# Attention and feed-forward block on one core: two tiles of exponentials in one ScalarE instruction where no dense item holds a bank, and a rearranged end

## The chip, the cores and the metric

The kernel runs on one core of one Trainium2 chip. The core has five engines with queues of their own: TensorE (PE, the matrix engine), VectorE (DVE), ScalarE (ACT), GpSimd (POOL) and SyncE (SP, which issues the DMAs). The matrix engine writes into PSUM, which has eight banks of 512 fp32 values on each of 128 partitions. The metric is the device time of one execution in microseconds; three runs of the kernel before gave a median of 1225.08 us (1224.64 to 1225.44).

## The reference

A pre-norm block on 2048 tokens of width 512. Attention has 32 heads of 16 columns; the feed-forward part is 1792 wide. All inputs are bfloat16.

```python
x = A_x                                    # (1, 2048, 512)
# attention on layernorm(x)
scores = einsum("bhqd,bhkd->bhqk", q, k) * 16 ** -0.5
p = softmax(scores);  o = einsum("bhqk,bhkd->bhqd", p, v)
h  = x + o.reshape(B, S, D) @ wo
# feed-forward on layernorm(h)
h2 = h + (gelu(hn @ w_gate) * (hn @ w_up)) @ w_down
```

The scores are 32 x 2048 x 2048 values, 134 million. Each of them is written into PSUM twice: once so that its row's maximum can be taken, and once more, shifted by that maximum, for the exponential.

## The kernel before, in words

**Two passes over the scores.** The work is cut into 64 units of four heads and 256 queries (or eight heads and 128 queries in the last 16 units), and each unit into 16 steps, called ticks. In one tick, pass one has PE write two banks of raw scores (`p1_pair`, L852, two matmuls of 512 columns) and DVE take the row maxima of both banks in one instruction of 1024 columns (`p1_consume`, L867). Pass two is 24 ticks behind, on a unit whose maxima are known. In the same tick PE writes two tiles of shifted scores, one bank each (`p2_tile`, L943, two or four matmuls for a tile), and ACT takes one exponential per tile, 128 x 512 from PSUM to a ring of 34 bf16 tiles in SBUF, called PTM, PTE and PTG (`p2_consume`, L972). Later PE multiplies these tiles with the values (`item_pv`, L989), ACT copies the sums out (OB), and a DMA and GpSimd finish the division.

**Fourteen units take one tick less.** In the units listed in `JOINT`, the maxima of the last two key chunks of one pair are taken together: PE writes a difference of scores into a bank (`item_diff`, L1075 and L1077), ACT takes its relu into SBUF (RB, L1080), and DVE adds it back while it reduces (L864, twice in such a unit). One tick of pass one falls away.

**Dense items run beside it.** Projections, the output projection, the gate, up and down matmuls and the PV sums are generators in a list. The class `Dense` takes one at a time and advances it by a piece or so per tick. An item holds one PSUM bank from its start until its result has been copied out, most often by ACT (`evac_act`, L696). In a tick with no dense work PE gets two filler matmuls instead (`dummy`, L1587).

**Banks.** Pass one uses banks 0 to 3 in two pairs. Pass two and the dense items share banks 4 to 7 through a first-in, first-out list, `banks.free`. A tile takes the bank at the front; when the instruction that reads it is written down, the bank goes to the back of the list. In the program a bank can thus be handed on before its reader has run, and PE waits for that reader by a semaphore.

**Order and waits.** The Python program writes down, tick by tick, one list of instructions for each engine. Each engine executes its list strictly in order. Waits are worked out from what each instruction reads and writes. The two matmuls of pass one and the first tile of pass two are one group (`group_begin`, `group_end`): all their waits are moved ahead of the group's first matmul. In a tick, PE's list is: the group, the second tile, then the dense piece or the fillers. ACT's list is: the exponentials, then the copy of a dense item that has just ended, then whatever was deferred (tanh, squares).

**The planner's costs.** `act_lag` is an account of how far ACT should be behind. Each tick adds 0.478 us per exponential and subtracts 1.135; a copy adds 0.48. Dense items start, and the tanh instructions are placed, only while the account is low enough (`LAG_START`, `LAG_OP`, `LAG_TH`). Nothing of it waits at run time: it sets the order alone.

**The end.** When pass one is over (tick 1024), the last 40 or so tiles of exponentials are done in pairs, 128 x 1024 in one instruction (`p2_pair`, L960). Then `tail_b` finishes the last token tile: the division, output projection, second norm, gate and up with the hardware's gelu, and down.

Of the kernel before, what the change touches and what calls it, by code (L numbers as in the profile page):

```python
# [209 lines left out]
ACT = mybir.ActivationFunctionType  # L210
# [5 lines left out]
NFC = F // 128  # L216
# [5 lines left out]
PV_T = (15, 16, 17, 18)  # L222
PV_TL = (9, 10, 17, 18)
DOWN_AT = 2
A_LATE = True
GH = 6
# [13 lines left out]
J_AT, J_GONE = 10, 14  # L240
LAG_EXTRA = 0.3
POLY = 1.3
TICK = 1.135
# [4 lines left out]
def bass_sequential_preLN__mha_block__geglu_ffn__prompt_kernel(nc, A_x, A_wqkv, A_wo, B_x, B_w_gate, B_w_up, B_w_down, out):  # L248
    dbg = None
    with ExitStack() as es:  # L250
# [288 lines left out]
        class Dense:  # L539
            def __init__(self):  # L540
                self.prio = []
                self.ready = []
                self.extra = []
                self.gen = None
                self.bank = None
                self.banks = [7, 3, 4, 5]
                self.rr = 0
                self.pause = 0
                self.single = False
                self.done = 0  # L550
                self.now = 0
# [15 lines left out]
            def piece(self):  # L567
                if self.single and self.pause > 0:
                    return 0
                while True:  # L570
# [17 lines left out]
                    try:  # L588
                        cost = next(self.gen)
                        if isinstance(cost, tuple):  # L590
                            if self.single:
                                self.pause = cost[1]
                            if ticking[0]:
                                return 0
                            continue
                        return cost
                    except StopIteration as fin:
                        self.gen = None
                        self.done += 1
                        if self.single:  # L600
                            banks.give(self.bank)
                            self.pause = 0 if dve_free[0] else PAUSE
                        return fin.value
            def busy(self):
                return bool(self.gen is not None or self.ready or self.prio)
# [10 lines left out]
        def defer(k, fn):  # L616
            deferred.append((dense.now + k, fn))
# [330 lines left out]
        def p2_pair(ui, tiles):  # L948
# [12 lines left out]
            else:  # L961
                for b, pi in ((b0, q0), (b1, q1)):
                    P.op("act", lambda e, b=b, pi=pi: e.activation(out=PTt(pi), in_=pbank[:, b, :], func=ACT.Exp), reads=[("pb", b)], writes=[("PT", pi)])

        def p2_consume(ui, tiles):
            for (b, m, g) in tiles:
                pi = pt_n[0] % NPT; pt_n[0] += 1
                assert pi not in pt_busy, "PT ring too small"
                pt_busy.add(pi)
                pt_of[(ui, m, g)] = pi  # L970
                dX = rdeps("M", [(n_, i_) for n_ in ("QKE", "QKE2") for i_ in range(5)]) if NPT_M - 10 <= pi < NPT_M else rdeps("E", [("xn", t) for t in range(NT)]) if NPT_M <= pi < NPT_M + NPT_E else (rdeps("G", [("x", cc) for cc in range(NCH)]) if pi >= NPT_M + NPT_E else ())
                P.op("act", lambda e, b=b, pi=pi: e.activation(out=PTt(pi), in_=pbank[:, b, :], func=ACT.Exp), reads=[("pb", b)], writes=[("PT", pi)], extra_deps=dX)  # L972
                banks.give(b)
# [216 lines left out]
        def item_oprojA(b):  # L1190
# [7 lines left out]
            P.op("pe", lambda e: e.matmul(pbank[:, b, :], ident[:], hh, start=False, stop=True), reads=["ident", ("h", GL % 2, 0)], writes=[("pb", b)], sig=True)  # L1198
            P.op("dve", lambda e: e.bn_stats(out=stats2[:, t, :], in_=pbank[:, b, :]), reads=[("pb", b)], writes=[("stats2", t)])
            P.op("dve", lambda e: e.tensor_copy(out=hh, in_=pbank[:, b, :]), reads=[("pb", b)], writes=[("h", GL % 2, 0)])  # L1200
            P.op("dve", lambda e: e.bn_aggr(out=mv2[:, t, :], in_=stats2[:, t, :]), reads=[("stats2", t)], writes=[("mv2", t)])
            P.op("dve", lambda e: e.tensor_scalar(out=rstd2[:, tt], in0=mv2[:, tt, 1], scalar1=EPS, scalar2=None, op0=ALU.add), reads=[("mv2", t)], writes=[("rstd2", t)])
# [7 lines left out]
        def item_hnA(b):  # L1210
            pt = pbank[:, b, :].bitcast(BF16)
            for dc in range(4):
                P.op("pe", lambda e, dc=dc: e.transpose(out=pt[:, 128 * dc:128 * dc + 128], in_=hn_sb[:, 0, 128 * dc:128 * dc + 128], identity=ident[:]),
                     reads=[("OH", 0), "ident"], writes=[("pb", b)], sig=(dc == 3))
            P.op("dve", lambda e: e.tensor_copy(out=hnT_l[GL % 2][:, :, 0:128], in_=pt[:, 0:512].rearrange("p (c s) -> p c s", c=4)), reads=[("pb", b)], writes=[("hnT", GL % 2, 0)])
            add_raw()
            return 1
            yield
# [299 lines left out]
        def tail_b():  # L1518
# [7 lines left out]
            for t in range(NTL):  # L1526
                raw_gelu(t)
            raw_mult(0)
            while not a_done[0]:
                fill(1)  # L1530
# [12 lines left out]
            P.op("pool", lambda e: e.tensor_tensor(out=rstd2[:, tt], in0=rstd2[:, tt], in1=nhalf[:, 0:1], op=ALU.pow), reads=[("rstd2", t1), "nhalf"], writes=[("rstd2", t1)])  # L1543
            raw_mult(1, "dve")
            raw_mult(2)
            raw_mult(3)
            P.op("dve", lambda e: e.tensor_scalar(out=hn_sb[:, 1, :], in0=g_h(GL, 1), scalar1=mv2[:, t1, 0:1], scalar2=rstd2[:, tt], op0=ALU.subtract, op1=ALU.mult),
                 reads=[("h", 1, 1), ("mv2", t1), ("rstd2", t1)], writes=[("OH", 1)])
            down_h(0, GL, 0)
            for fc in chunks(0):  # L1550
                down_mm(0, GL, 0, fc)
            fill(FILL_A)
            tail_hnT(2, (0, 1), "act")
            tail_hnT(3, (2, 3), "dve")
            for fc in chunks(1):
                down_mm(0, GL, 0, fc)
# [6 lines left out]
            for t in range(NTL):  # L1563
                tail_gate(gb[2 * t % 5], t)
                tail_up(gb[(2 * t + 1) % 5], t)
                if t == 0:
                    for fc in range(8, NFC):
                        down_mm(0, GL, 0, fc)
                    P.op("act", lambda e: e.activation(out=out_sb[:, 0, :], in_=pbank[:, 0, :], func=ACT.Copy), reads=[("pb", 0)], writes=[("osb", 0)])
                    P.dma("sp", lambda e: e.dma_start(out=outv[:, 2 * GL, :], in_=out_sb[:, 0, :]), ("out", 0), reads=[("osb", 0)], writes=[("outd", 2 * GL)])  # L1570
# [33 lines left out]
        ticking[0] = True  # L1604
        def next_tile():
            n = 2 * t2 - behind[0]
            st, jj = n // 2, n % 2
            ui_ = st // 16
            t = p2_tile(ui_, st % 16, 1 - (st + P2_START) % 2, jj)
            return ui_, t  # L1610
        while True:
# [37 lines left out]
            else:  # L1649
                t1 = p1_pair(tick // 16, tick % 16, gp1) if p1_ok else []  # L1650
                if doubles[0]:
                    p1_next.append(p1_pair((tick + 1) // 16, (tick + 1) % 16, 1 - gp1))
            t2l = [next_tile()] if p2_ok and p1_ok else []
            P.group_end("pe")
            if p2_ok and p1_ok:
                behind[0] -= 1
                t2l.append(next_tile())
                if more:
# [15 lines left out]
            if t1:  # L1674
# [5 lines left out]
                if tick == 16 * NU - 1:  # L1680
                    unit_end(tick // 16)
            for ui_, t in t2l:
                p2_consume(ui_, [t])
# [34 lines left out]
            tick += 1  # L1718
        run_deferred(tick, flush=True)
        dense.now = tick + 16  # L1720
        while len(pv_done) < NU:
# [36 lines left out]
```

## Time and profile before

| what | value |
|---|---|
| median of three runs | 1225.08 us |
| the profiled execution | 1225.74 us, span 1224.0 us |
| ACT busy | 1190.3 us, 97% of the span |
| DVE busy | 1181.1 us, 96% |
| PE busy | 1130.3 us, 92% (774 of its matmuls are fillers) |
| POOL busy | 841.3 us, 69% |
| DVE row maxima, 128 x 1024 (L867) | 996 |
| ACT exponentials 128 x 512 (L972) | 2000 |
| ACT exponentials 128 x 1024 (L960), all after pass one | 22 |

The page counts an instruction from its start to its end. Where instructions of one engine overlap, the mean of a group is longer than the time from one end to the next, and the engine can follow one on another faster than that mean. The chain of waits shows the latter: it lists the pieces of the chain that ended last, in order of time, and leaves the overlap out. "Idle before" of a group is the time in which the engine stood still ahead of its instructions, with what ended it.

### The profile page before, as it was taken

How to read it: one execution, taken by the hardware profiler on the slowest of the kernel's cores; microseconds unless marked ns; L12 is line 12 of the kernel's file. 1: busy time of each engine (PE TensorE's matmuls, PEld its weight loads, DVE VectorE, ACT ScalarE, POOL GpSimd, SP SyncE). 2: the span in 40 equal slices, each digit the busy share in tenths (PEclk: the TensorE clock that was granted, in tenths of full speed). 3: DMA queues.
4: the chain of work that ended last, by engine and by line, in shares of the span. 5: the costliest groups of instructions: out<-in, count | busy, mean ns of one | idle time of the engine just before them, and what ended most of it. 6: DMA issues, size and time to landing. Idle time of an engine off the chain costs nothing.

```text
span 1224.0 us, 36091 instructions
## 1 busy us (share of the span) xinstructions
PE 1130.3 (92%) x14845; PEld 476.7 (39%) x14845; DVE 1181.1 (96%) x1124; ACT 1190.3 (97%) x2421; POOL 841.3 (69%) x1774
## 2 busy tenths in 40 slices
PE   7999998899999999999999999999999999999998
PEld 3233232233333333333332333333334455554565
DVE  8999999999999999999999999999999999999963
ACT  7899999999999999999999999999999999999995
POOL 8567684766776676756868487675767687756762
PEclk9999999999999999999999999999999999999999
DMA  5111104300010000110011000100001100010000
GB/s 153 28 34 27 29 24 136 91 10 9 8 28 21 12 11 8 27 25 8 11 25 14 21 8 10 25 21 15 8 10 27 26 20 13 10 27 13 18 20 15
DMA packets 69651, 32.02 MB, mean 26 GB/s; under 512 B 54768, under 2 KB 68464, under 8 KB 69488
## 3 DMA queue, kind: packets, MB, share of 16 engines
q1 hardware_dynamic: 69488, 29.71, 10.0%
q8 instruction: 118, 1.93, 0.7%
q14 instruction: 45, 0.37, 0.1%
HBM read 11.80 MB, written 2.10 MB: 11 GB/s over the span
## 4 chain that ended last, share of the span: by engine, by line
ACT 56%; DVE 32%; PE 8%; issue 2%; DMA 1%; POOL 1%; POOLq 0%; DVEq 0%
ACT PTM L972 32%; DVE PM L867 31%; ACT PTG L972 10%; ACT PTE L972 5%; PE pbank L1391 2%; ACT th_sb L1262 2%; ACT g_sb L696 2%; ACT u_sb L696 2%; PE pbank L943 1%; PE pbank L852 1%; ACT PTM L960 1%; ACT OB L696 1%; PE pbank L1292 1%; PE pbank L1587 1%; DVE OA L864 1%
## 5 line engine op out<-in xcount | busy, mean ns | idle before, releaser
L867 DVE TENSOR_REDUCE PM<-pbank 128x2 f32<-128x1024 f32 x996 | 1134.9, 1213 | 9.3 <-PE pbank L943 4.4
L972 ACT ACTIVATE PTM<-pbank 128x512 bf16<-128x512 f32 x1357 | 733.0, 718 | 4.4 <-PE pbank L943 1.0
L943 PE MATMUL pbank<-QT,KT 32*128 32x256 bf16 (+1 forms) x5120 | 506.2, 250 | 14.6 <-ACT PTM L972 8.1
L852 PE MATMUL pbank<-KT,QT 32*128 32x512 bf16 x2020 | 388.2, 384 | 25.4 <-DVE PM L867 10.0
L1587 PE MATMUL pbank<-ones_bf,ident 128*128 128x512 bf16 x774 | 237.0, 384 | 29.2 <-ACT PTM L972 4.7
L852 PEld LDWEIGHTS pbank<-KT,QT 32*128 32x128 bf16 x2020 | 97.2, 91 | 351.1 <-DVE PM L867 130.2
L943 PEld LDWEIGHTS pbank<-QT,KT 32*128 32x128 bf16 x5120 | 205.9, 92 | 69.0 <-ACT PTM L972 40.1
L972 ACT ACTIVATE PTG<-pbank 128x512 bf16<-128x512 f32 x407 | 225.1, 710 | 0.8 <-PE pbank L943 0.4
L972 ACT ACTIVATE PTE<-pbank 128x512 bf16<-128x512 f32 x236 | 140.3, 719 | 1.0 <-PE pbank L943 0.7
L989 PE MATMUL pbank<-PTM,VA 128*17 128x256 bf16 (+1 forms) x3470 | 126.0, 252 | 1.6
L1030 POOL TENSOR_TENSOR LINV<-OBT,negone 128x8 f32<-128x8 bf16 x63 | 105.1, 1668 | 6.2 <-DMA OBT<-OB 5.9
L1587 PEld LDWEIGHTS pbank<-ones_bf,ident 128*128 128x128 bf16 x774 | 45.3, 97 | 132.6 <-ACT PTM L972 83.8
L1272 POOL TENSOR_TENSOR th_sb<-g_sb 128x512 f32<-128x512 f32 (+1 forms) x50 | 51.2, 1024 | 63.6 <-ACT g_sb L696 63.6
L989 PEld LDWEIGHTS pbank<-PTM,VA 128*17 128x17 bf16 x3470 | 67.1, 90 | 39.8 <-issue 22.1
L1271 POOL TENSOR_TENSOR th_sb<-th_sb,g_sb 128x512 f32<-128x512 f32 (+1 forms) x50 | 62.4, 1248 | 4.0
L922 POOL TENSOR_TENSOR QT<-QT,STG 128x256 bf16<-128x256 bf16 x64 | 42.8, 668 | 31.8 <-DMA STG<-ST 31.1
L1274 POOL TENSOR_TENSOR th_sb<-th_sb,g_sb 128x512 f32<-128x512 f32 (+1 forms) x50 | 62.3, 1246 | 1.7
L1270 POOL TENSOR_SCALAR th_sb<-th_sb 128x512 f32<-128x512 f32 (+1 forms) x50 | 30.5, 611 | 40.9 <-ACT th_sb L1262 40.7
L1391 PE MATMUL pbank<-wd_sb,GUT 128*128 128x512 bf16 x210 | 57.4, 382 | 1.0 <-DVE OnT L1422 0.3
L767 POOL TENSOR_SCALAR QT<-QKS,qmask 128x512 bf16<-128x512 bf16 x30 | 46.9, 1568 | 13.3 <-ACT QKS L696 11.9
L1347 PE MATMUL pbank<-hnT_l,wg_sb 128*128 128x256 bf16 x336 | 51.2, 275 | 3.3 <-ACT PTM L972 0.7
L1383 POOL TENSOR_TENSOR GUT<-th_sb,u_sb 128x512 bf16<-128x512 f32 x42 | 53.3, 1268 | 1.3
(198 smaller groups left out, 1210.1 us busy)
## 6 DMA issues: line engine op xcount, KB each, us to landing
QKS<-QKS SPq DMA_DIRECT2D x27, 112.0 KB, 2.1
x_sb<-in_A_x_dram SPq DMA_DIRECT2D x4, 512.0 KB, 5.8
xres<-in_A_x_dram SPq DMA_DIRECT2D x16, 128.0 KB, 2.4
out_dram<-out_sb SPq DMA_DIRECT2D x15, 128.0 KB, 1.7
wg_sb<-in_B_w_gate_dram SPq DMA_DIRECT2D x4, 448.0 KB, 4.2
wu_sb<-in_B_w_up_dram SPq DMA_DIRECT2D x4, 448.0 KB, 3.9
wd_sb<-in_B_w_down_dram SPq DMA_DIRECT2D x3, 512.0 KB, 4.5
STG<-ST SPq DMA_TRANSPOSE x64, 2.3
```

What stands on the lines that cost most here:

```text
L696: P.op("act", lambda e: e.activation(out=o_ap, in_=i_ap, func=ACT.Copy, **kw), reads=reads, writes=writes, extra_deps=extra)
L852: P.op("pe", lambda e, g=g, b=b: e.matmul(pbank[:, b, :], QT[32 * g:32 * g + 32, c, slot, 128 * qt:128 * qt + 128], KT[32 * g:32 * g + 32, ...
L867: P.op("dve", lambda e: e.tensor_reduce(out=PM[:, par, qt, kc, g:g + 2], in_=pbank[:, b:b + 2, :], axis=AX.X, op=ALU.max), reads=[("pb", b ...
L943: P.op("pe", lambda e, kt=kt, i=i: e.matmul(pbank[:, b, qn * i:qn * i + qn], KT[32 * g:32 * g + 32, slot, 128 * kt:128 * kt + 128], QT[32 ...
L972: P.op("act", lambda e, b=b, pi=pi: e.activation(out=PTt(pi), in_=pbank[:, b, :], func=ACT.Exp), reads=[("pb", b)], writes=[("PT", pi)], e ...
L989: P.op("pe", lambda e, g=g, kt=kt, pi=pi, i=i, s_=s_, c0=c0, qn=qn: e.matmul(pbank[32 * g:32 * g + 17, b, c0:c0 + qn], VA[:, kt, 4 * s_ + ...
L1030: P.op("pool", lambda e: e.tensor_tensor(out=li, in0=o4[:, :, :, 16], in1=negone[:, 0:4 * nq].rearrange("p (q h) -> p q h", q=nq), op=ALU. ...
L1271: o(1.27, lambda e: e.tensor_tensor(out=ts_, in0=ts_, in1=gs, op=ALU.mult), [("th", par), ("g", par)])], then=done)
L1274: o(1.27, lambda e: e.tensor_tensor(out=ts_, in0=ts_, in1=gs, op=ALU.mult), [("th", par), ("g", par)])], then=poly_done)
L1383: P.op("pool", lambda e: e.tensor_tensor(out=o_ap, in0=shp(ts_), in1=shp(us), op=ALU.mult), reads=[("th", par), ("u", par)], writes=o_keys ...
L1391: P.op("pe", lambda e: e.matmul(pbank[:, b, :], GUT[:, fc, 128 * k:128 * k + 128], wd_sb[:, fc, :], start=first, stop=last), reads=[("GUT" ...
L1587: P.op("pe", lambda e: e.matmul(pbank[:, b, :], ident[:], ones_bf[:, 0:512], start=True, stop=True), reads=["ident", "ones_bf"], writes=[( ...
```

## The change

Five things change.

1. **Pairs of exponentials during pass one.** If no dense item holds a bank when a tick begins, and two neighbouring banks are both in the free list (`pair_banks`), the two tiles of the tick are put into these two, and one ACT instruction of 128 x 1024 reads both (`p2_both`). Where the two places in the ring of SBUF tiles are not side by side, two single instructions are written as before. `pair_banks` looks for the first bank in the list whose neighbour is anywhere in the list.
2. **The planner's account.** Each pair takes 0.05 us off `act_lag` (`PAIR_GAIN`), so that dense items and tanh instructions may be placed earlier.
3. **A second dense item beside a waiting one.** After pass one, when the running item can't go on, another ready item may run next to it (`beside`).
4. **The last unit's sums and the first of the two last token tiles.** The third and fourth PV part of the last unit may start at ticks 14 and 17 instead of 17 and 18. In `item_oprojA` the copy of h comes before the statistics, which now read the copy in SBUF. The raw gate and up items are added one tick later (`defer(1, add_raw)`).
5. **The order in `tail_b`.** One piece of dense work is placed between the ticks and the end (`TAIL_P`). GpSimd multiplies parts 0 and 1 first; DVE takes part 2, and part 3 after the transposes. The down matmuls of the second last token tile are 8, then 4, then 2, where they were 4, 4 and 6.

```diff
-PV_TL = (9, 10, 17, 18)
+PV_TL = (9, 10, 14, 17)
+TAIL_P = 1
+PAIR_GAIN = 0.05
...
                         if isinstance(cost, tuple):
+                            if dve_free[0]:
+                                other_cost = self.beside()
+                                if other_cost:
+                                    return other_cost
...
+        def pair_banks():
+            for b in banks.free:
+                if b ^ 1 in banks.free:
+                    return b & 6
+            return None
+
+        def p2_both(tl):
+            (ua, (b0, ma, ga)), (ub, (b1, mb, gb)) = tl
+            n = pt_n[0] % NPT
+            if n + 1 < NPT and pt_tiles[n][0] is pt_tiles[n + 1][0] and b1 == b0 + 1:
+                (q0, d0), (q1, d1) = place(ua, ma, ga), place(ub, mb, gb)
+                o_ap = pt_tiles[q0][0][:, pt_tiles[q0][1]:pt_tiles[q0][1] + 2, :]
+                P.op("act", lambda e: e.activation(out=o_ap, in_=pbank[:, b0:b0 + 2, :], func=ACT.Exp), reads=[("pb", b0), ("pb", b1)], writes=[("PT", q0), ("PT", q1)], extra_deps=d0 + d1)
+                banks.give(b0)
+                banks.give(b1)
+                act_lag[0] = max(0.0, act_lag[0] - PAIR_GAIN)
+            else:
+                for u_, t_ in tl:
+                    p2_consume(u_, [t_])
...
-            P.op("dve", lambda e: e.bn_stats(out=stats2[:, t, :], in_=pbank[:, b, :]), reads=[("pb", b)], writes=[("stats2", t)])
             P.op("dve", lambda e: e.tensor_copy(out=hh, in_=pbank[:, b, :]), reads=[("pb", b)], writes=[("h", GL % 2, 0)])
+            P.op("dve", lambda e: e.bn_stats(out=stats2[:, t, :], in_=hh), reads=[("h", GL % 2, 0)], writes=[("stats2", t)])
...
-            add_raw()
+            defer(1, add_raw)
...
             raw_mult(0)
+            raw_mult(1)
...
-            raw_mult(1, "dve")
-            raw_mult(2)
-            raw_mult(3)
+            raw_mult(2, "dve")
...
-            for fc in chunks(0):
+            for fc in range(8):
                 down_mm(0, GL, 0, fc)
             fill(FILL_A)
             tail_hnT(2, (0, 1), "act")
             tail_hnT(3, (2, 3), "dve")
-            for fc in chunks(1):
+            raw_mult(3, "dve")
+            for fc in chunks(2):
                 down_mm(0, GL, 0, fc)
...
-                    for fc in range(8, NFC):
+                    for fc in chunks(3):
                         down_mm(0, GL, 0, fc)
...
-            t2l = [next_tile()] if p2_ok and p1_ok else []
+            pb_ = pair_banks() if p2_ok and p1_ok and dense.gen is None and True else None
+            t2l = [next_tile(pb_)] if p2_ok and p1_ok else []
             P.group_end("pe")
             if p2_ok and p1_ok:
                 behind[0] -= 1
-                t2l.append(next_tile())
+                t2l.append(next_tile(None if pb_ is None else pb_ + 1))
...
+            if pb_ is not None:
+                p2_both(t2l[:2])
+                t2l = t2l[2:]
             for ui_, t in t2l:
                 p2_consume(ui_, [t])
```

## The prediction

> **What bounds the kernel now.** I read the page first, then the groups of pass one's stretch, then the chain of waits in order of time. Durations are in us.
>
> ```profile
> PE 1130.3 (92%) x14845; PEld 476.7 (39%) x14845; DVE 1181.1 (96%) x1124; ACT 1190.3 (97%) x2421; POOL 841.3 (69%) x1774
> PEclk9999999999999999999999999999999999999999
> ACT 56%; DVE 32%; PE 8%; issue 2%; DMA 1%; POOL 1%; POOLq 0%; DVEq 0%
> ```
>
> Two engines are full, and the chain goes to and fro between them. DVE's part, asked for from 33.2 (the first of an unbroken row of maxima) to 1177.8 (the last one's end):
>
> ```profile
> L867 DVE TENSOR_REDUCE PM<-pbank 128x2 f32<-128x1024 f32 x984 | 1120.9, 1213 | 8.4 <-PE pbank L943 4.4 <-PE pbank L852 0.8
> L864 DVE CUSTOM_DVE_ANT_0 OA<-pbank,OA 128x512 f32<-128x512 f32 x28 | 18.1, 682 | 0.1
> ```
>
> The unit prices stand in the chain:
>
> ```profile
> 49.40 1.96 ACT PTM L972 x4
> 571.86 0.28 ACT OB L696
> 645.74 34.01 DVE PM L867 x30
> 1188.81 3.66 ACT PTM L960 x4
> ```
>
> A row maximum takes 34.01/30 = 1.13, a single exponential 0.49, a copy of PV sums (OB) 0.28, an exponential over two banks 3.66/4 = 0.915. Copies of gate, up and the relu RB also cost 0.49, a tanh 0.51. The stretch is 1144.6 long, and DVE's work in it is 984 x 1.131 + 28 x 0.608 = 1130.0. So **ACT and PE together hold DVE up by 14.6, and no relief of ACT can give back more than that.** A full unit is 16 x 1.131 = 18.10 of DVE, a joint unit 17.05.
>
> I summed the same by unit, from the order of instructions and these prices, for units 1 to 63: DVE 1125.4, ACT 1118.0, the larger of the two in each unit 1135.1. The trace has 1140.0, so a unit takes what its fuller engine needs, plus 0.08.
>
> What a wait of PE costs its followers is in two more pieces of the chain:
>
> ```profile
> 644.71 0.05 issue
> 644.75 0.60 PE pbank L1587 x2
> 645.36 0.22 PE pbank L852
> 645.58 0.17 PE pbank L943 x3
> ...
> 683.24 0.05 issue
> 683.29 0.30 PE pbank L852
> 683.59 0.36 PE pbank L943 x5
> 683.95 2.54 ACT PTM L972 x5
> ```
>
> In the second, PE's group is released at 683.24 and ACT begins 0.71 later; its five exponentials take 2.54, not 5 x 0.49 = 2.45, so the first costs 0.09 more when ACT stood idle. In the first piece two fillers stand ahead, and DVE starts 1.03 after the release; without them it is about 0.45 to 0.5.
>
> **The change part by part.** *Pairs.* The order of instructions of the changed kernel has 542 pairs in pass one (1084 of 2000 tiles). Each saves 2 x 0.49 - 0.916 = 0.064, in all 34.4 of ACT; with what moves between the engines at the end, ACT's units sum to 1085.1, not 1118.0. With nothing else changed, the larger sums of the units come to 1131.0: only 4 gained, as DVE needs nearly that anyway, and as the account (`PAIR_GAIN`) fills the freed time of many units with dense work that came later before.
>
> The Trainium skill puts another price on the pair: "ScalarE: Activation LUTs", section "What ACT_TABLE_LOAD costs", gives an ACTIVATE 186 ns plus 0.833 ns an element, with 93 ns of overlap back to back. That is 0.520 and 0.946 (an estimate from that page of the Trainium skill), a saving of 0.093, where the rows show 0.49 and 0.915; by it the forecast below would be some 7 lower. I keep the rows.
>
> *The wait that it adds.* Before, a tile takes the bank at the front of the list, so ACT always has two or three instructions (0.98 or more) left to run between the one that freed the bank and the one that needs it refilled. `pair_banks` takes the first bank whose neighbour is free too, and that neighbour may be the bank handed back last. When a dense item has just ended, it is the bank whose copy ACT has not yet done. The order shows it. Tick 170 of the changed kernel ends with ACT's OB copy of bank 6, and tick 171's group opens with a wait for that copy, because it takes banks 6 and 7; before, bank 6 went to tick 172. Counting all ticks, the instruction that frees the bank stands *directly* ahead of the exponential that needs it 124 times (never before): 62 after an OB copy, 28 after a relu RB, 24 after an exponential, 10 after other copies. Nearly all are waits of the group. Queued behind it on PE are both banks of pass one, both tiles and the dense piece; DVE waits for the first, ACT for the second. POOL's maxima and the DMAs follow DVE's step and have slack (POOL is at 69%).
>
> Cost on ACT, if it is the fuller engine: 0.71 + 0.09 = 0.80 from the row, whose group fed a third tile; for two I take 0.75. Nothing can hide it, because ACT has no other instruction in its list. 124 x 0.75 = 93.
>
> Cost on DVE, if ACT is ahead. The group of a step is released by the reduce two steps back; the reduce between covers 1.13 less the path of 0.5 and a start of 0.1, so a slack of 0.5. Counted from the release of the step before, exponentials begin at 0.71, two singles end at 1.78, OB at 2.06. That is 0.93 after the next reduce's end and overshoots the slack by 0.4. A relu behind a pair ends at 0.71 + 1.01 + 0.49 = 2.21, overshoots by 0.58, and when a second follows two steps later the loop (relu, tiles, pair, the other step's pair, relu) is 0.71 + 1.01 + 0.92 + 0.49 = 3.13 against 2.26, 0.87 lost; mean 0.7. After an exponential: 0.1. Others: 0.5. Sum 62 x 0.4 + 28 x 0.7 + 24 x 0.1 + 10 x 0.5 = 51.
>
> *Smaller waits.* 133 further pairs have only one single (0.49) between, and wait 0.1 to 0.27 if ACT is full; 170 have one pair between, and up to 0.28 where fillers stand in the path. A full ACT pays them, an early one does not: 0 to 27 more.
>
> *Dense items.* Number and kind stay; fillers go from 774 to 775. PE gains and loses nothing.
>
> *The end.* After the transposes of the last tile PE has 9 down matmuls and one residual where it had 4, and later 2 where it had 6: 2 x 0.215 = +0.4 on PE's chain to the end. ACT's two idle gaps at 1182 and 1184 (0.40 and 0.48, waiting for L943 behind raw gate matmuls) can go: up to -0.9. DVE's last product and GpSimd's second lie beside other work (POOL is idle from 1199.9 to 1203.9 and DVE for 2.6 after 1209.9). The statistics take 0.59 from SBUF (L395 at 5.94) and 0.70 from PSUM (L1199 at 1179.44): 0.1 at most. I take 0 in all, with ends -2 and +2, a lost tail gap on each side.
>
> **Sum.** For each unit I take the larger of DVE's work plus its stalls and ACT's work plus 0.75 an event: 1205.7 against 1135.1 before, +70.6. If a unit may hand up to 1.0 of ACT's lateness to the next (the slack above, twice), both fall, to 1193.6 and 1127.8: +65.8. I take the latter, as units heavy and light for ACT alternate. The sum is made against the span of 1224.0 in an execution of 1225.74, 0.66 above the median; on the median it is 1225.1 + 66 = 1291.
>
> **The rivals.**
>
> *DVE's stalls alone (ACT always early).* 1125.4 + 51 = 1176.9, +37 against 1140.0 or +42 by the account: 1262 to 1267. For it: long stretches of the chain are DVE alone (34.01 at 645.74). Against: ACT is at 97%, and half the units have 17.4 or more of its work after the change as well.
>
> *The small waits all count.* The account with 0.2, 0.1 and 0.05 for them gives 1233.0, +98: 1323. For it: ACT at the limit never catches up, as a pair with fillers in its path needs 0.05 + 0.60 + 0.5 + 1.0 per two steps, near DVE's own pace. Against: most fall into units where DVE is slower.
>
> *The other side: pairs win.* If copies end so early that the group never waits for them, the 14.6 of DVE's idle time come back, at best 1210; by the account 4, so 1221. It takes a price under 0.04 an event for the account's 4 (124 x 0.04 = 5), or under 0.12 for the whole 14.6. Speaking for it: the planner places copies where ACT has room. Against: the row of 0.71, which is PE's own path and not a matter of room.
>
> *The matrix clock falls.* PE would stand still for 0.5 or so 124 times. If its clock halved for three steps at each, 0.99 of PE work a step would become 1.98 against 1.13: 124 x 3 x 0.85 = 316, 1541. The row PEclk is 9 in all slices, with PE gaps of 0.4 to 0.7 in them already. The Trainium skill, "TensorE: Matmul & The Clock Gate", section "A second HAM failure mode: psum-queue depth-cycling", tells of short idle times between groups that made the clock swing; by that rule this could come, and no row here shows it.
>
> **How the numbers follow.** About 0.2% (2.5 us) can be told from no change. Forecast (+55 to +80) 0.50; DVE's stalls alone 0.22; all small waits 0.19; pairs win 0.05; no change, gains and waits cancelling, 0.02; the clock 0.02. The range goes from 1250 (two thirds of DVE's stalls) to 1325 (all small waits). Faster 0.05, same 0.02, slower 0.93.
>
> **What would show it.** Right: a group L1010 of 542 at a spacing near 0.92; ACT's busy sum falling by 20 or more though the span grows; DVE's idle time before its maxima (L892) up from 9 to 50 or more, released by PE's L877; waits of PE's L877 on ACT's OB (L721) and RB (L1129) that were not there; in the chain OB, then L877, L968, then DVE or ACT. Wrong: L877 waiting for ACT no longer than now, or a pair's spacing over 0.98, which would put the loss on the instruction itself; or a clock below 9.

## The result and the profile after

The changed kernel takes 1384.8 us (median of 4 runs, 1383.3 to 1385.4). The kernel before took 1225.3 us beside it (1224.6 to 1225.9). The ratio is 1.130, with an interval of 1.128 to 1.131: 160 us slower, where 66 were forecast. The profiled execution is 1384.8 us with a span of 1383.1. The end is not the place of it: from the end of the last row maximum (1338.2) to the end of the span it takes 44.9 us, and it took 46.2 before. The loss lies in pass one. From here on durations are in us.

The steps below are the ticks of the kernel's description. The page of the changed kernel, with the engines, the clock that PE was granted, and the shares of the chain of waits:

```profile
PE 1110.1 (80%) x14700; PEld 458.9 (33%) x14846; DVE 1206.0 (87%) x1122; ACT 1221.3 (88%) x1882; POOL 841.7 (61%) x1773
PEclk9999999999999999999999999999999999999999
ACT 59%; PE 36%; issue 3%; DVE 2%; POOL 0%; POOLq 0%
```

The trace lacks the records of 146 of PE's matmuls (14700 against 14846 weight loads), so PE's 80% is a few points low. No engine is full any more. DVE has nearly left the chain (32% before, 2% now), and PE, the least busy of the three, has 36% of it where it had 8%. That is what a ring of waits looks like: each engine stands still while another one does a short thing for it.

The groups of the changed kernel: instructions, busy time and mean ns, then the idle time just ahead of them and what ended it.

```profile
L892 DVE TENSOR_REDUCE PM<-pbank 128x2 f32<-128x1024 f32 x996 | 1160.0, 1217 | 143.7 <-PE pbank L968 136.8
L877 PE MATMUL pbank<-KT,QT 32*128 32x512 bf16 x2020 | 397.5, 394 | 137.5 <-ACT OB L721 52.0
L1010 ACT ACTIVATE PTM<-pbank 128x1024 bf16<-128x1024 f32 x401 | 398.4, 1023 | 67.6 <-PE pbank L968 61.8
```

DVE stood still for 9 ahead of its row maxima before; now it is 144. The maximum needs the raw scores of L877, which wait for ACT's copies: 137.5 idle ahead of L877, 52.0 of it ended by the OB copy, in the view of waits in 62 places.

```profile
PE pbank L877 <- ACT OB L721: 52.0, 62, 1.3
PE pbank L877 <- ACT OA L1129: 24.6, 27, 1.3
```

The second line is the relu (RB in the prediction; the trace shows it by its line, L1129). One such place, from the chain in order of time (start, length, what):

```profile
405.84 0.29 ACT OB L721
406.12 0.05 issue
406.17 0.28 PE pbank L877
406.45 0.21 PE pbank L968 x3
406.66 0.02 issue
406.68 1.02 ACT PTM L1010
407.71 0.50 ACT OA L1129
408.21 0.05 issue
408.25 0.28 PE pbank L877
408.54 0.21 PE pbank L968 x3
408.74 0.02 issue
408.77 1.03 ACT PTM L1010
```

ACT's copy ends at 406.12, PE fills the bank, ACT starts again at 406.68: it stands still for 0.55, and the pair that follows takes 1.02 because it begins on an idle engine. One behind the other a pair takes 0.92. (In "581.25 1.90 ACT PTM L1010 x2" of the same chain the first takes about 0.98 and the second 0.92.) One step later the same happens with the relu.

**Where the 160 went.** From the trace's semaphore events I took, for each ACT instruction of pass one (steps 24 to 1023), the time from the end of the instruction before it to its own end, less its price (0.49, 0.9165 and so on). What is left is time that ACT loses, whether idle or in a slow start.

| ahead of the exponential, since its bank was last read | count | lost, total | mean |
|---|---|---|---|
| nothing: the freeing instruction is directly ahead | 124 | 87.7 | 0.71 |
| a pair, 0.3 to 0.8 of ACT's work between | 133 | 19.8 | 0.15 |
| a pair, 0.92 between | 170 | 22.7 | 0.13 |
| a single, 0.92 between | 169 | 20.5 | 0.12 |
| a single, 0.98 to 1.3 between | 370 | 27.3 | 0.07 |
| a single, 0.3 to 0.8 between | 197 | 13.3 | 0.07 |
| all others | | 20.0 | |
| sum after | | 211.3 | |
| sum before | | 18.5 | |

ACT loses 192.8 more than before and has 33 less work to do: 160, the whole loss. Such an account comes out for any engine that is at work from one end of pass one to the other. That ACT and PE, and not DVE, set the time is read from the chain above (59%, 36% and 2%), and experiment 4 tries it. 88 of ACT's lost time are the waits that the prediction counted; some 105 more are smaller ones.

These smaller ones are of two kinds. For each exponential I also took the waits in PE's list up to its tiles and noted which of them ended last. Where under 0.9 of ACT's work lies between, it is ACT's own reading of the bank, and 33.1 is lost in 330 places. Where 0.92 or more lies between, 84.3 is lost, and 67.5 of it where the last wait was for DVE's row maximum (15.3 of 18.7 before). ACT had read those banks long before; its tiles are late because they stand in PE's list behind L877, which waits for DVE. And in places with 54.4 of the 67.5 (1.5 of the 15.3 before), one of the last three row maxima had itself ended more than 0.05 behind DVE's pace of 1.131. That is the order of events if a delay goes from ACT to DVE and back to ACT; which wait began each was not followed up.

### The profile page after: what moved, and what is told of

It is laid out like the page before. It is cut to its first block, busy times and chain, and to the rows that moved or that the text cites. A ratio compares the mean times of both kernels' runs of the same rounds, so it can differ in the third digit from the quotient of the medians.

```text
span 1383.1 us, 35370 instructions
## 1 busy us (share of the span) xinstructions
PE 1110.1 (80%) x14700; PEld 458.9 (33%) x14846; DVE 1206.0 (87%) x1122; ACT 1221.3 (88%) x1882; POOL 841.7 (61%) x1773
## 4 chain that ended last, share of the span: by engine, by line
ACT 59%; PE 36%; issue 3%; DVE 2%; POOL 0%; POOLq 0%
ACT PTM L1010 20%; ACT PTM L1021 15%; PE pbank L968 10%; PE pbank L877 9%; ACT PTG L1021 6%; ACT PTG L1010 5%; PE pbank L1636 5%; ACT PTE L1021 4%; PE pbank L1038 3%; PE pbank L1440 3%; ACT PTE L1010 2%; ACT th_sb L1311 2%; DVE PM L892 2%; PE pbank L1396 1%; ACT OB L721 1%
## 5 line engine op out<-in xcount | busy, mean ns | idle before, releaser
L892 DVE TENSOR_REDUCE PM<-pbank 128x2 f32<-128x1024 f32 x996 | 1160.0, 1217 | 143.7 <-PE pbank L968 136.8
L968 PE MATMUL pbank<-QT,KT 32*128 32x256 bf16 (+1 forms) x5120 | 508.8, 255 | 46.2 <-ACT PTM L1010 25.1
L877 PE MATMUL pbank<-KT,QT 32*128 32x512 bf16 x2020 | 397.5, 394 | 137.5 <-ACT OB L721 52.0
L1010 ACT ACTIVATE PTM<-pbank 128x1024 bf16<-128x1024 f32 x401 | 398.4, 1023 | 67.6 <-PE pbank L968 61.8
L1021 ACT ACTIVATE PTM<-pbank 128x512 bf16<-128x512 f32 x555 | 308.1, 597 | 28.1 <-PE pbank L968 25.3
L1636 PE MATMUL pbank<-ones_bf,ident 128*128 128x512 bf16 x663 | 219.0, 401 | 50.2 <-ACT PTM L1010 27.4
L877 PEld LDWEIGHTS pbank<-KT,QT 32*128 32x128 bf16 x2020 | 95.0, 91 | 480.9 <-issue 123.8
L968 PEld LDWEIGHTS pbank<-QT,KT 32*128 32x128 bf16 x5120 | 187.2, 93 | 114.4 <-ACT PTM L1010 62.1
L1021 ACT ACTIVATE PTG<-pbank 128x512 bf16<-128x512 f32 x207 | 116.2, 599 | 5.9 <-PE pbank L968 5.4
L1010 ACT ACTIVATE PTG<-pbank 128x1024 bf16<-128x1024 f32 x100 | 100.9, 1025 | 19.7 <-PE pbank L968 17.5
L1321 POOL TENSOR_TENSOR th_sb<-g_sb 128x512 f32<-128x512 f32 (+1 forms) x50 | 51.2, 1023 | 91.5 <-ACT g_sb L721 91.4
L1021 ACT ACTIVATE PTE<-pbank 128x512 bf16<-128x512 f32 x154 | 88.6, 599 | 7.7 <-PE pbank L968 6.9
L907 POOL TENSOR_TENSOR MX<-PM,MX 128x8 f32<-128x8 f32 x64 | 13.0, 204 | 78.9 <-DVE PM L892 78.0
L920 POOL TENSOR_TENSOR MX<-PM,MX 128x8 f32<-128x8 f32 x64 | 12.9, 202 | 73.8 <-DVE PM L892 73.5
```

What stands on the lines that cost most here:

```text
L877: P.op("pe", lambda e, g=g, b=b: e.matmul(pbank[:, b, :], QT[32 * g:32 * g + 32, c, slot, 128 * qt:128 * qt + 128], KT[32 * g:32 * g + 32, ...
L892: P.op("dve", lambda e: e.tensor_reduce(out=PM[:, par, qt, kc, g:g + 2], in_=pbank[:, b:b + 2, :], axis=AX.X, op=ALU.max), reads=[("pb", b ...
L968: P.op("pe", lambda e, kt=kt, i=i: e.matmul(pbank[:, b, qn * i:qn * i + qn], KT[32 * g:32 * g + 32, slot, 128 * kt:128 * kt + 128], QT[32 ...
L1010: P.op("act", lambda e: e.activation(out=o_ap, in_=pbank[:, b0:b0 + 2, :], func=ACT.Exp), reads=[("pb", b0), ("pb", b1)], writes=[("PT", q ...
L1321: pool.add([o(1.04, lambda e: e.tensor_tensor(out=ts_, in0=gs, in1=gs, op=ALU.mult), [("g", par)], dE), o(0.62, lambda e: e.tensor_scalar( ...
L1636: P.op("pe", lambda e: e.matmul(pbank[:, b, :], ident[:], ones_bf[:, 0:512], start=True, stop=True), reads=["ident", "ones_bf"], writes=[( ...
```

## The experiments

The edits are to the changed kernel, unless it is said otherwise. Times are medians, and each ratio is to the kernel before on the same chip.

**1. The end alone.** No pair is ever formed in pass one; all else stays.

```diff
-            pb_ = pair_banks() if p2_ok and p1_ok and dense.gen is None and True else None
+            pb_ = pair_banks() if p2_ok and p1_ok and dense.gen is None and False else None
```

> The changed kernel with pairing in pass one switched off (pair_banks is never asked), so that only the rearranged end and the second dense item beside a waiting one are left. If the whole loss comes from the pairs: 1223 to 1228 us, within 2 us of the kernel before, and ACT's idle time before its exponentials as small as before. If the rearranged end has a share in the loss: over 1230 us, with the extra time after the last row maximum.

Measured: 1224.25 against 1225.78, ratio 0.9987 (0.9979 to 0.9996). The page's shares of the chain and DVE's group:

```profile
ACT 54%; DVE 35%; PE 7%; issue 2%; POOL 1%; DMA 1%
L892 DVE TENSOR_REDUCE PM<-pbank 128x2 f32<-128x1024 f32 x996 | 1134.6, 1212 | 8.9 <-PE pbank L968 4.3
```

DVE's idle time is back at 9, and ACT loses 17.9. The whole loss belongs to the pairs, to the banks chosen for them and to `PAIR_GAIN`, which comes into force only with a pair and was not tried alone. The rearranged end is worth about 1.5, and this version is the only one here that is faster than the kernel before, by less than the 0.2% that the forecast took as its bound.

**2. The banks of the pairs, but single exponentials.** `pair_banks` chooses as in the change; each of the two tiles is read by its own instruction and hands its bank back at its own end.

```diff
-            if n + 1 < NPT and pt_tiles[n][0] is pt_tiles[n + 1][0] and b1 == b0 + 1:
+            if False:
```

> The changed kernel with the banks chosen as pair_banks chooses them, but two exponentials of 128x512 always, never one of 128x1024. 116 exponentials follow directly on the instruction that frees their bank. Theory A (the choice of banks makes PE wait for a copy not yet done, 0.7 us each): 116 x 0.7 = 81 more than the kernel before, about 1300 us. Rival B (an exponential over two banks hands both back at its end only, and PE and ACT then take turns): without such instructions 1235 us or less. Both together: between.

Measured: 1335.37, ratio 1.088 (1.086 to 1.090), 35 more than theory A gave. Without one paired instruction in pass one, 111 of the loss are there (1335.4 - 1224.3). Group and wait:

```profile
L892 DVE TENSOR_REDUCE PM<-pbank 128x2 f32<-128x1024 f32 x996 | 1153.7, 1216 | 105.3 <-PE pbank L968 94.3
...
PE pbank L877 <- ACT OB L721: 51.5, 57, 1.3
```

The wait for the OB copy has hardly changed (51.5 in 57 places). ACT loses 134.3, of which 78.3 are in 116 places with the freeing instruction directly ahead, 0.675 each, and 21.3 in 154 places with one instruction of 0.3 to 0.6 between, which the expectation did not count. So the order in which banks are handed out is a cause by itself.

**3. Pairs only from the two oldest banks.** A pair is formed only if the two banks at the front of the list are neighbours.

```diff
-            for b in banks.free:
-                if b ^ 1 in banks.free:
-                    return b & 6
-            return None
+            o = sorted(banks.free[:2])
+            return o[0] if len(o) == 2 and o[1] == o[0] + 1 else None
```

> The changed kernel with a pair only where the two banks longest in the free list are neighbours: 255 pairs, and no exponential follows directly on the instruction that frees its bank. Theory A: the 0.7 us waits are gone; with the smaller waits at the means of the changed kernel's trace (0.07 to 0.13 each, 45 in all) against 18 before and 16 of ACT's work saved, about 1236 us. Rival B, in proportion to the pairs (255 of 542, of a loss of 160 us): about 1300 us. Rival C (PE's clock falls because PE stands still, and this is much of the loss): the clock is back at 1.0 if the waits are gone.

Measured: 1243.22, ratio 1.014 (1.013 to 1.016), 7 more than theory A gave. 255 pairs are left, and no exponential stands directly behind the instruction that frees its bank. ACT still loses 55.6. DVE's group:

```profile
L892 DVE TENSOR_REDUCE PM<-pbank 128x2 f32<-128x1024 f32 x996 | 1142.1, 1214 | 23.3 <-PE pbank L968 16.7
```

The big waits are gone and it is still 19 slower than without pairs (1224.3): 0.074 per pair, on top of the 0.064 that each saves ACT. Smaller waits are a price of their own. Of the 55.6, only 8.9 stand at banks with under 0.9 of ACT's work since their last reading; 33.4 stand where PE's last wait was for DVE.

**4. Pass one not held up by the bank of the pair.** When a pair is coming, the group is closed before its first tile, so L877 no longer waits for ACT.

```diff
+            if pb_ is not None:
+                P.group_end("pe")
             t2l = [next_tile(pb_)] if p2_ok and p1_ok else []
-            P.group_end("pe")
+            if pb_ is None:
+                P.group_end("pe")
```

> The changed kernel with PE's group closed after the two matmuls of pass one in the steps with pairs, so that these no longer wait for ACT, only the tiles do. Theory A with ACT as the fuller engine: the wait of the tiles stays (release to tiles 0.45 instead of 0.58 us), so 124 x 0.13 = 16 us less than the changed kernel, about 1368 us. If DVE's late start (136.8 us of idle time before its maxima) is what sets the time, most of the loss goes: under 1300 us.

Measured: 1370.56, ratio 1.117 (1.115 to 1.119). Only 14 come back, as theory A has it (1368). The waits:

```profile
DVE PM L892 <- PE pbank L968: 67.9, 153, 1.7
...
DVE PM L892 <- PE pbank L877: 41.3, 125, 1.1
```

L877 comes earlier in its step, but the tile behind it (L968) now stands at the wait, and all that follows in PE's list, the next step's L877 among it, stands behind that tile. DVE's wait is handed on by one step. So DVE's late start within the step was not what set the time; of the 143.7 that DVE stands idle ahead of its maxima, 117.0 are left here.

**5. Fillers off the path.** The prediction put the waits of 170 pairs, "up to 0.28", down to fillers ahead of the tiles. In steps of pass one fillers now write a bank of pass one, not a bank that ACT has just read.

```diff
-                dummy(next(b for b in ((6, 7) if doubles[0] else banks.free) if dense.gen is None or b != dense.bank), want - (cost or 0))
+                dummy(2 * (p1_ring[0] % 2) if p1_ok and p2_ok else next(b for b in ((6, 7) if doubles[0] else banks.free) if dense.gen is None or b != dense.bank), want - (cost or 0))
```

> The changed kernel with the two filler matmuls of a step written to the bank that pass one uses next, so that they wait for DVE and no longer for ACT. If the fillers stand in the path from a pair's end to the tiles of the second next step, the waits of the 339 exponentials with one pair between (43 us of ACT's idle time) shrink to a quarter: about 1350 us. If the fillers run beside the wait anyway: within 5 us of 1385. The clock tells whether PE is then busy at better times: over 0.974.

Measured: 1395.82, ratio 1.139 (1.137 to 1.140), 11 more than the change where 35 less were expected. DVE's group and the shares of the chain:

```profile
L892 DVE TENSOR_REDUCE PM<-pbank 128x2 f32<-128x1024 f32 x996 | 1161.6, 1219 | 152.8 <-PE pbank L968 144.6
...
ACT 53%; PE 31%; DVE 12%; issue 3%; DMA 0%; POOL 0%
```

The fillers now wait for DVE's reduce instead of ACT's exponential, and DVE's share of the chain goes from 2% to 12%. Refuted: the fillers were not the cause, or what they cost is only moved to the other bank. In the changed kernel's trace a filler's wait is the last one of PE ahead of an exponential in 5 places, with 1.5 lost.

**6. Pairs without the direct waits.** A pair may not take a bank that ACT's last written instruction reads; all else as in the change, and again 542 pairs.

```diff
+        if eng == "act":
+            self.last_act = [b[1] for b in reads if b[0] == "pb"]
...
-                if b ^ 1 in banks.free:
+                if b ^ 1 in banks.free and b not in P.last_act and b ^ 1 not in P.last_act:
```

> The changed kernel, but pair_banks passes over a bank that the instruction written last for ACT still has to read. There are again 542 pairs, and no exponential follows directly on the instruction that frees its bank (124 before); 311 have one single exponential or copy between instead, where it was 330, and 446 have one pair between, where it was 339. Theory A: the 124 waits (87.7 us of ACT's idle time in the changed kernel's trace) go, and some 107 pairs take the smaller wait of 0.15 (16 us): about 1313 us, and the clock nearer to 1.0. Rival B (pairs as such cost, whatever stands before them): within 20 us of 1385.

Measured: 1317.23, ratio 1.074 (1.072 to 1.076), against 1313 expected. By this edit 68 of the 160 come back, and 92 remain without a direct wait (L894, L970 and L1012 are the lines L892, L968 and L1010 of the changed kernel):

```profile
L894 DVE TENSOR_REDUCE PM<-pbank 128x2 f32<-128x1024 f32 x996 | 1156.5, 1218 | 80.8 <-PE pbank L970 73.4
...
L1012 ACT ACTIVATE PTM<-pbank 128x1024 bf16<-128x1024 f32 x401 | 398.5, 1023 | 29.7 <-PE pbank L970 21.5
```

Of the 142.9 that ACT loses here, 48.9 stand ahead of the 240 pairs with one other instruction in between (0.204 each), 23.5 ahead of the 213 pairs with one pair, 0.92, between (0.11), and most of the rest ahead of singles, 27.2 of it at 0.98 to 1.3 between (349 x 0.078). In the change the same two kinds of pairs are those that the prediction had down as "0 to 27 more". In 54 of the 240 the instruction between is an OB copy of 0.28, and these lose 16.7, or 0.31 each: the edit takes the direct waits away, but it still hands out banks that were read a moment ago. So it is in part luck that the time came within 4 of what was expected. The 240 pairs lose 29 more than the 133 of the change, where 16 were expected. The counts differ too: singles included, 444 exponentials have one single or copy between and 430 one pair, not 311 and 446.

**7. What the clock alone does.** In the kernel before, the fillers of the steps of pass one are left out; nobody reads what they write. The banks of the work stay as they were, and no wait is added.

```diff
-            if (cost or 0) < want:
+            if (cost or 0) < want and not (p1_ok and p2_ok):
```

> The kernel before without its filler matmuls in the steps in which both passes run (766 fewer of 804). No bank is chosen otherwise and no wait is added, so what changes is PE's idle time alone. Theory C (idle time between PE's groups makes the clock fall, and a step at half clock takes 1.7 us, as 43 steps of the changed kernel's trace did): the clock falls below 0.97 and the time rises by 0.4 us for each such step, 20 us or more. If the clock stays at 1.0: 1220 to 1226 us, and the idle time of the waits alone has not set the clock in the changed kernel either.

Measured: 1277.94, ratio 1.043 (1.040 to 1.046): 52 slower with 766 weight loads, and as many filler matmuls, less to do. Its granted clock, in tenths by slice, and DVE's group (L867 and L943 as in the kernel before):

```profile
PEclk9988886678877988779867888778887989897999
...
L867 DVE TENSOR_REDUCE PM<-pbank 128x2 f32<-128x1024 f32 x996 | 1143.1, 1215 | 52.2 <-PE pbank L943 47.3
```

The mean clock is 0.849. Steps at half clock take 1.28, the others 1.16, so such a step costs 0.12 here and not the 0.4 that was expected. 58.7 of the 71.3 that ACT loses in this run lie in the stretches at half clock. So a lower clock by itself stops DVE and ACT in the same way, and the question is how much of it the changed kernel has; this is taken up below.

**8. Experiments 3 and 5 together.** Pairs from the two oldest banks, fillers in a bank of pass one, `PAIR_GAIN` 0 (the edits of experiments 3 and 5, and `PAIR_GAIN = 0.0`).

> A try at a version that is faster than both: the changed kernel with pairs only on the two banks longest free where these are neighbours, no gain entered in the planner's account, and the fillers written to pass one's next bank. By the smaller waits of the run with pairs on the longest free banks (55.6 us of ACT's idle time, 18 of them there before; some 12 behind fillers) and 16 of ACT's work saved: 1225 to 1235 us. Below 1222 it would beat the kernel before and the one with no pairs.

Measured: 1248.83, ratio 1.019 (1.017 to 1.020), at a clock of 1.0, 14 above the range that was expected. It is no better than experiment 3 alone; ACT loses 58.6.

**9. Pairs only where both banks have long been read.** The program counts ACT's work as it writes it down, and a pair is formed only if at least 0.9 of it has been written since the last reader of both banks.

```diff
+        if eng == "act":
+            nb = sum(1 for b in reads if b[0] == "pb")
+            self.act_work += 0.92 if nb == 2 else 0.49
+            self.read_at.update({b[1]: self.act_work for b in reads if b[0] == "pb"})
...
-                if b ^ 1 in banks.free:
+                if b ^ 1 in banks.free and all(P.act_work - P.read_at.get(x, -9.0) > 0.9 for x in (b, b ^ 1)):
...
```

A third place, not shown, leaves out a step's fillers when no bank is free for them.

> The changed kernel with a pair only where ACT has at least 0.9 us of other work written after the last reader of each of the two banks: 173 pairs, 81 of them with one pair or less than 0.98 us between, none with less. If a pair costs what its banks' age leaves uncovered: 173 x 0.064 = 11 us of ACT's work saved against some 0.05 to 0.07 us of wait a pair and a little more before the singles: 1225 to 1240 us, less than the 1243 of the 255 pairs on the longest free banks. If a pair costs the same at any age (93 us for 542 in the run without direct waits, 0.17 each): 1224 + 29 = 1253 us.

Measured: 1238.07, ratio 1.010 (1.008 to 1.012), clock 1.0. A second run has the same without the second dense item beside a waiting one:

```diff
-                            if dve_free[0]:
+                            if False:
```

> The same pairs as in the run with 173 pairs on banks that ACT read long ago, with the second dense item beside a waiting one switched off, so that the order after pass one is the usual one. Pass one is the same in both, so 1234 to 1242 us; the per-pair price of that run then holds.

Measured: 1240.14, ratio 1.012 (1.010 to 1.013). In both kernels 14 down matmuls of one of the 16 token tiles stand so late that they read products of the next tile, so that this tile's output differs; no work is left out. But the order of the dense work after pass one is another one here: from the end of the last row maximum to the end of the span the two take 50.2 and 52.0, where experiment 1 takes 44.9. So 5 to 7 of the loss do not lie in pass one. There the first of them is 9.3 longer than experiment 1 (last maximum at 1186.3 against 1177.0): each of the 173 pairs costs 0.05 more than it saves. With 255 pairs it was 0.074 and with the 542 of experiment 6 it was 0.17. Of the 40 that ACT loses in pass one, 3.8 stand at banks with under 0.9 of its work since their last reading. No selection of pairs that was tried beats no pairs.

**The two causes side by side.** Four of these kernels make a square:

| | no direct waits | with direct waits |
|---|---|---|
| single exponentials | 1224 (exp. 1) | 1335 (exp. 2) |
| 542 pairs | 1317 (exp. 6) | 1385 (the change) |

Bank choice alone costs 111, and both together 160. The 93 of experiment 6 are not the price of pairs alone, since 63.9 of what ACT loses there stands at banks with under 0.9 of its work since their last reading; single exponentials on just these banks were not run. 111 and 93 add up to more than 160, which fits that a step which already stands at a big wait does not pay a small one as well; that was not measured apart.

## Why the prediction was right in kind and too low

*Place and sign.* Right. The loss is in pass one, at banks that are handed on before ACT has read them, and the chain shows OB, L877, L968, L1010 as forecast. Pairs do not come out ahead anywhere.

*124 direct waits at 0.75, 93 in all.* Right within 6%: 124 places lost 87.7, 0.71 each. Taking them away gave 68 and not 88 to 93 (experiment 6), since that edit leaves more pairs with one short instruction in between (240 where the change has 133).

*"A full ACT pays them, an early one does not: 0 to 27 more."* **This step failed**, together with the next one. It was the term of the small waits. I counted 303 pairs and put nothing for them into the sum. The runs show 42.5 in these 303 places, and 61.1 ahead of single exponentials with one or two instructions between, which I had not counted at all; before, all small losses came to 18.5. By what ended PE's wait, 33.1 of the new loss is at banks with under 0.9 of ACT's work since their last reading. A pair reads two banks and gives both back only at its end, so the first bank comes back some 0.4 later than after a single. That this makes the next refill late is argued from the program; no run gives the two banks back apart. (The 133 pairs that I described as having one single between have a dense item's copy there.)

*The sum over units, "the larger of DVE's work plus its stalls and ACT's work plus 0.75 an event".* This failed too, and it is the larger part of the error (94 in all, at most 33.1 of it at banks that ACT had just read): it lets the work of the fuller engine hide the waits of the other. In the 36 units in which ACT is the fuller one by the account, it gave 714.4 and the trace has 778.0. In the other 26, where DVE should have hidden ACT's waits, it gave 472.6 and the trace has 502.3. What the account lacks is the way back: in those 36 units ACT lost 23.8 where PE's last wait was for DVE, and 1.5 in the same units before; in the 26 units it is 43.7 against 13.8. ACT cannot work ahead there, because its tiles stand in PE's list behind L877, which waits for DVE. So the larger of the two would have to be taken by step and not by unit; no account by step was made. Not all of the 52 that ACT loses more behind DVE is loss of time, as ACT also has 33 less to do. (The sum of DVE's stalls comes to 51.8 by its terms, not 51, which changes nothing.)

*The 14.6 as the bound of any gain, ACT's saving of 34.4.* The saving is there (33 by the trace's prices, 0.0635 a pair) and by the account it went mostly into units that DVE fills. But the mark that I gave for it was wrong: ACT's busy sum did not fall by 20, it rose from 1190.3 to 1221.3. The page counts an instruction from start to end, and a pair on an idle engine counts 1.02 to 1.03 where it takes 0.92 behind another. The spacing of pairs was as forecast.

*The end, 0 between -2 and +2.* Right: experiment 1 puts it at -1.5, and the change's own tail is 1.3 shorter.

*The rivals.* DVE's stalls alone (1262 to 1267) fell short, and experiment 4, which starts L877 earlier, gave only 14 back. It does not refute them by itself, since it hands DVE's waits on more than it takes them away. "The small waits all count" (1323) came nearest. It had the price of the pairs about right: 0.2 for 133 and 0.1 for 170 make 44, and 42.5 was lost there. What it lacked is the same as above, the singles and the way back through DVE. The clock, at 0.02, came in part. The changed kernel has 14 stretches at half clock, 71.7 long in all, the kernel before had none until its end. Two windows of the changed kernel, the first one of these stretches (length; busy time and count of PE, weight loads, DVE, ACT, POOL; granted clock):

```profile
300.30:307.10 6.80, 6.32 (x35) 1.47 (x33) 4.86 (x5) 4.65 (x6) 2.51 (x4) 0.50 0.00 0
375.40:382.20 6.80, 5.70 (x80) 2.39 (x78) 6.09 (x6) 6.74 (x11) 4.17 (x5) 1.00 0.00 0
```

At 0.50 PE is busy for 6.32 of 6.80 with less than half of the matmuls. The row PEclk of the page shows 9 throughout, since one of its slices is 34.6 long; such a stretch is seen only in narrower windows. 43 steps lie in such stretches and take 1.69, the others 1.29: 43 x 0.40 = 17 of the 160. This estimate puts the whole difference down to the clock; with the 0.12 of experiment 7 it would be 5. All that ACT loses inside these stretches is 24.8. No run gave the changed kernel its full clock. Experiment 6 points the same way: its clock is 0.996 and 92 of the loss are still there. The feared 316 did not come, because the clock fell in 14 places and not at each of 124 waits.

Singles with 0.98 to 1.3 of work between lose 0.074 each in the changed kernel and 0.017 before. Here too 26.5 of the 27.3 stands where PE's last wait was for DVE, and 0.8 in the other 224 places.

Left open: how the clock's share and the waits' share divide within one step, what `PAIR_GAIN` does alone, and by which waits the pairs of experiments 3 and 9 cost their 0.05 to 0.074 when so little is lost at banks that were just read.

## What to carry to other kernels

Where engines run in lockstep through a handful of banks, hand banks out by age, and count for every refill how much work its reader still has between freeing a bank and needing it again; an exponential that needed a bank again at once lost 0.71 here, and one with 0.3 to 0.8 of work between still 0.07 to 0.15. In a program like this one, where an instruction's end is its one signal, an instruction that reads two banks hands the first one back only when it is through with the second; here the pairs cost 0.05 to 0.17 each, after the 0.064 of start time that each saved. When adding up stalls, ask how far two engines can really run apart, which is what the buffers between them allow, before one engine's work is counted as hiding the other's waits; and price the many small waits as well as the few big ones.

## What the runs showed that I had not expected

The clock that PE is granted fell to 0.50 in stretches of 3.41 or 6.83, although between 40 and 1330 PE never stood still for more than 1.31 in the changed kernel and was about 80% busy over the span. The Trainium skill, "TensorE: Matmul & The Clock Gate", section "What's actually happening", has the clock fall after an idle window of some 3.4; the lengths of the stretches agree with such a window, but here no gap came near it. In the Trainium skill, the same page's section "A second HAM failure mode: psum-queue depth-cycling" tells of short idle times that are enough, and the trace agrees with that one. At 92% busy (before) the clock held through pass one, and without most of the fillers, at 86% by the page, it fell to a mean of 0.849. The busy share alone does not say it, since the changed kernel, with the lowest, has 0.974. The 766 filler weight loads and their matmuls, which compute nothing, are thus worth 52 to the kernel before.

A wait's price on ACT was nearly the same wherever it stood directly behind the freeing instruction: 0.714 for pairs, 0.66 for singles, 0.675 with singles only (experiment 2). It consists of about 0.55 for PE's two matmuls of 512 columns and the tiles behind them, and 0.1 to 0.14 for an instruction that starts on an idle ACT.
